# Two blocks of 96 columns of an fp32 MLP product made together from three packed weight sets

## The chip, the cores and the metric

The kernel runs on one core of a Trainium2 chip. The metric is the device time of one execution in microseconds (us); each version is run several times, and the median counts. A core has five engines that run side by side, each with its own queue of instructions: TensorE (matmuls, PE in the profile, with its weight loads as PEld), VectorE (DVE), ScalarE (ACT), GpSimd (POOL) and SyncE (SP), which issues most transfers from memory. Data lies in SBUF, with 128 partitions, and matmul results lie in PSUM, which is eight banks here used as four slots of two banks.

## The reference

The reference has two halves. The first gates a long causal convolution (a diagonal state space model) with the queries and adds it to the input. The second, which matters here, is a token-mixing MLP on 2048 tokens and 640 channels with F = 1728 hidden columns:

```python
h = _layernorm(x, axis=-1)                            # (B, S, D), then scaled and shifted
u = jnp.einsum("bsd,sf->bdf", h, w1) + b1             # 2048 tokens -> 1728 columns
u = _gelu(u)
y = jnp.einsum("bdf,fs->bds", u, w2) + b2             # 1728 columns -> 2048 tokens
```

All of it is in fp32. The change touches only the first of these two products.

## The kernel before

**Three matmuls for one.** TensorE is fed with the type fp32r, and each fp32 operand is split into a rounded high part and the rest ("lo"). The helper `mm` (L437 to L444) makes high x high, high x rest and rest x high, each in two halves of 320 columns: six matmuls of 128x128 weights for one block of 128 columns and one 128-token chunk. The product of the two rests is left out. The tokens come in 16 chunks `H[j]`, each a pair (high, rest) of 640 columns, so one block takes 96 matmuls.

**The blocks.** The 1728 hidden columns are cut into 14 blocks of 128, seven for each half of 864. Since 864 is six times 128 and 96 more, blocks 6 and 13 repeat 32 columns of the block before them and have 96 new ones (`fo`, L384). When such a block's result leaves PSUM, the mask `msk` sets its first 32 rows to zero (L850, L851).

**The order.** The program's order is written out by hand; waits follow from which tiles are read and written. Blocks 0 to 3 are made earlier, beside the second layer norm, in four accumulators. Then the loop at L899 runs over blocks 4 to 13. For each it first splits the next block's weights (`split_w`, L423: two ScalarE copies for the high part, L432, and two VectorE subtractions for the rest) and loads the one after that (`load_w`, L396: two transfers of 512 KB on SP), then issues the 96 matmuls, then the evacuation `u_evac` (L844): a gelu in place in PSUM on ScalarE (L847), and for each half of 320 columns a ScalarE copy and a VectorE subtraction into the tiles `U[f]`. Loads go into one raw tile `X`; split weights go into two tiles `T_wb` in turn, by the block's parity.

**The tiles.** A tile name stands for a place in SBUF, and a new tile in a place waits for all uses of the old one. The place "in" holds block 3's weights until TensorE is through with blocks 0 to 3, and then `u_i`, where results go. The place "p" holds `m_p`, with room for temporaries. PSUM slots are taken in a ring of four.

**After it.** In the last block's time, VectorE and ScalarE make sums of the results for a Strassen-like second product (`t_ops`, L863, for three of seven parts), and only then evacuate block 13. The second product starts with a plain loop over four column blocks of w2 (L1029 to L1052), each with 14 groups of six matmuls, one for each `U[f]` in order of f, and then runs 42 smaller products (L974).

Of the kernel before, what the change touches and what calls it, by code (L numbers as in the profile page):

```python
# [10 lines left out]
F32R = mybir.dt.float32r  # L11
AF = mybir.ActivationFunctionType
ALU = mybir.AluOpType
# [37 lines left out]
def mixer_kernel(ctx: ExitStack, tc: tile.TileContext, q, k, v, shift_k, ssm_k, ssm_D, w1, b1, w2, b2, c,  # L51
# [7 lines left out]
    act, dve, pool, pe, sync = nc.scalar, nc.vector, nc.gpsimd, nc.tensor, nc.sync  # L59
    TT = lambda eng, o, a, b, op: eng.tensor_tensor(o, a, b, op=op)  # L60
    uid = [0]

    def mem(tag, n, name=None):

        return sb.tile([128, n], F32, name=name or tag, tag=tag, bufs=1)
# [4 lines left out]
    def psum(slot=None):  # L70

        uid[0] += 1
        slot = ring[uid[0] % len(ring)] if slot is None else slot
        return psp.tile([128, 1024], F32, name=f"pst_{uid[0]}", tag=f"pst{slot}", bufs=1)

    def dram(t, offset, ap):
        return bass.AP(tensor=t.tensor, offset=t.offset + offset, ap=ap)
# [206 lines left out]
    def i1(half, slot=None):  # L284

        ps = psum(slot)
        for jj in range(8):
            for ri in range(2):
                for e in range(2):
                    p = slice(64 * e, 64 * e + 64)  # L290
                    for b in range(2):
                        n2 = 16 * b + 8 * half + jj
                        pe.matmul(ps[64 * b:64 * b + 64, 512 * e + 64 * jj:512 * e + 64 * jj + 64],  # L293
                                  V1[p, ri, n2], T2[p, :, 32 * ri + n2], start=ri == 0, stop=ri == 1)
        return ps
# [85 lines left out]


    NF, NW = 14, 4
    fo = lambda f: 864 * (f // 7) + min(128 * (f % 7), 736)  # L384
    raw, blk = {}, {}
    j16 = lambda t: t[:, 0:2048].rearrange("p (j m) -> p j m", j=16)
    f14 = lambda t: t[:, 0:1792].rearrange("p (f m) -> p f m", f=14)

    def load_w2(t, s, f0, n):

        for h in range(n // 7 or 1):
            o = 7 * h
            sync.dma_start(t[:, o:o + 6, :], dram(w2, fo(f0 + o) * S + 128 * s, [[S, 128], [128 * S, 6], [1, 128]]))
            sync.dma_start(t[:, o + 6, :], dram(w2, fo(f0 + o + 6) * S + 128 * s, [[S, 128], [1, 128]]))

    def load_w(i, t=X):  # L396
        if i >= NF + NW:
            return
        if i < NF:
            t = j16(t)  # L400
            for b in range(2):
                sync.dma_start(t[64 * b:64 * b + 64],
                               dram(w1, 16 * b * F + fo(i), [[32 * F, 64], [F, 16], [1, 128]]))
            raw[i] = (t, [slice(0, 8), slice(8, 16)])
        else:
            t = f14(t)
            load_w2(t, i - NF, 0, 14)
            raw[i] = (t, [slice(0, 7), slice(7, 14)])
# [12 lines left out]
            TT(dve, blk[f][1][:, j].bitcast(F32R), t[:, :, 128 * f:128 * f + 128], blk[f][0][:, j], ALU.subtract)  # L421

    def split_w(i, t2=None, eng=dve):  # L423
        if i >= NF + NW:
            return
        if t2 is None:
            t2 = T_wb[i % 2]
        view = j16 if i < NF else f14
        hi, lo = view(t2[:, 0:2048]), view(t2[:, 2048:4096])
        t, parts = raw.pop(i)  # L430
        for f in parts:
            act.activation(hi[:, f].bitcast(F32R), t[:, f], AF.Copy)  # L432
        for f in parts:
            TT(eng, lo[:, f].bitcast(F32R), t[:, f], hi[:, f], ALU.subtract)
        blk[i] = hi, lo

    def mm(ps, wh, wl, rh, rl, first, last, steps=None):  # L437

        m = wh.shape[-1]
        steps = steps or ((wh, rh), (wh, rl), (wl, rh))  # L440
        for i, (w_, r_) in enumerate(steps):
            for h in range(2):
                pe.matmul(ps[0:m, h, 0:320], w_.bitcast(F32R), r_[:, 320 * h:320 * h + 320].bitcast(F32R),  # L443
                          start=first and i == 0, stop=last and i == 2)  # L444
# [78 lines left out]
    for c in range(NC):  # L523
# [3 lines left out]
        for g in range(8):  # L527
            m_, a_ = f2(g)
# [35 lines left out]
        if c == 0:  # L564
# [3 lines left out]
            ps = psum()  # L568
# [45 lines left out]
        else:  # L614
# [6 lines left out]
            t = mem("in", 4288, "wb3")  # L621
# [4 lines left out]
        if c:  # L626
            dv(7 if cn is not None else 8)
            i2(0)
            if cn is None:
                mod_part(tap, 3, pl[3])  # L630
                i2(1, dve)
                t = mem("y", 4096, "wb2")
# [19 lines left out]
        for half in range(2):  # L652
            ps = i1(half)
# [15 lines left out]
        else:  # L669
# [3 lines left out]
    r_z, r_v = mem("z", 8192, "r_z"), mem("v", 4520, "r_v")  # L673
    unit = lambda t, n: [t[:, 1280 * i:1280 * i + 1280] for i in range(n)]
    H = (unit(r_z[:, 0:4096], 3) + unit(r_v, 3) + unit(mem("aux", 4096, "h_a"), 3)
         + unit(r_z[:, 3840:7680], 3))
# [14 lines left out]
    start = []  # L691
# [84 lines left out]
    ps = i1(1, s1)  # L776
# [34 lines left out]
    for pr in range(3, 8):  # L811
# [15 lines left out]
        if pr == 4:  # L827
# [5 lines left out]

    U = {}
    thirds = lambda t, n, o=0: [t[:, o + 320 * i:o + 320 * i + 320] for i in range(n)]
    u_i = mem("in", 4288, "u_i")
    left = [t_ for t, n in ((mem("t", 1280, "u_t"), 4), (mem("g", 1280, "u_g"), 4), (mem("kt", 1536, "u_k"), 4))
            for t_ in thirds(t, n)] + thirds(u_i, 1, 3840) + thirds(r_z, 1, 7680)
    right = thirds(mem("xb", 5120, "u_x"), 14)
    us = [left[2 * f:2 * f + 1] + right[2 * f:2 * f + 1] + left[2 * f + 1:2 * f + 2] + right[2 * f + 1:2 * f + 2]  # L840
          for f in range(7)]
    us += [thirds(t, 4, 1280 * i) for t in (u_i, mem("y", 4096, "u_y")) for i in range(3)]

    def u_evac(f, ps):  # L844
        u = U[f] = us[f] if f < 13 else [t[:, 320 * h:320 * h + 320] for t in H[15] for h in range(2)]
        p = ps[:, :, 0:320]
        act.activation(p, p, AF.Gelu_apprx_tanh, bias=B1C[:, f:f + 1])  # L847
        for h in range(2):
            if f % 7 == 6:
                act.activation(u[h].bitcast(F32R), p[:, h], AF.Copy, scale=msk)  # L850
                dve.scalar_tensor_tensor(u[2 + h].bitcast(F32R), p[:, h], msk, u[h], op0=ALU.mult, op1=ALU.subtract)  # L851
            else:
                act.activation(u[h].bitcast(F32R), p[:, h], AF.Copy)
                TT(dve, u[2 + h].bitcast(F32R), p[:, h], u[h], ALU.subtract)

    m_p = mem("p", 2048, "m_p")
    TU = [[(H[j][n][:, 0:320], H[j][n][:, 320:640]) for j in js for n in range(2)]
          for js in ((0, 1), (2, 6), (7, 8), (9, 10), (11, 12), (13, 14))]  # L860
    RB = thirds(m_p, 3, 1088)

    def t_ops(i, then=lambda: None):  # L863

        def whole(t, n, h):
            u = U[i + 7 * n]
            TT(dve, t, u[h], u[2 + h], ALU.add)
# [4 lines left out]
        def rest(n, t):  # L872
            TT(dve, TU[i][n][1].bitcast(F32R), t, TU[i][n][0], ALU.subtract)

        a, b, c_ = RB
        whole(a, 0, 0)
# [14 lines left out]
        rest(1, c_)  # L891
        rest(3, a)

    T_wb = [mem("w0", 4096, "wb0b"), mem("w1", 4096, "wb1b")]
    split_w(4)
    load_w(5)
    for f_ in range(4):
        u_evac(f_, acc[f_])
    for f_ in range(4, NF):  # L899
        ps = psum().rearrange("p (h m) -> p h m", h=2)  # L900
        split_w(f_ + 1)
        load_w(f_ + 2)
        for j in range(16):
            hh, hl = H[j]
            mm(ps, blk[f_][0][:, j], blk[f_][1][:, j], hh, hl, j == 0, j == 15)
        if f_ == NF - 1:
            m_v = mem("v", 4520, "m_v")
            for i in range(3):
                t_ops(i)
        u_evac(f_, ps)  # L910
# [4 lines left out]
    m_w, slots = [], []  # L915
# [105 lines left out]
    def early(s):  # L1021

        for h in range(2):
            o, x, b2_ = RB[h], xe[2 * s + h], B2C[:, s:s + 1]
            dve.scalar_tensor_tensor(o, acc[s][:, h, 0:320], b2_, GB[:, 320 * h:320 * h + 320], op0=ALU.add, op1=ALU.mult)
            TT(dve, x, o, x, ALU.add)
            sync.dma_start(out[128 * s:128 * s + 128, 320 * h:320 * h + 320], x)

    for s in range(NW):  # L1029
        i = NF + s  # L1030
        acc.append(psum().rearrange("p (h m) -> p h m", h=2))
        split_w(i + 1)
        load_w(i + 2)
        if s < 3:
            t_ops(3 + s)
        if s > 1:
            early(s - 2)
        if s == 3:
            load_pair(1, 0, 3)
            m_w.append(mem("w0", 4096, "m_w0"))  # L1040
            slots += [(q7(m_w[0], 1792 * i), q7(m_w[0], 1792 * i + 896)) for i in range(2)]
            prep(0)
            prep(1)
            sums(2)
            sums(3)
        wh, wl = blk[i]
        for f_ in range(NF):
            u = U[f_]
            for k, (w, r) in enumerate(((wh, 0), (wh, 2), (wl, 0))):
                for h in range(2):  # L1050
                    pe.matmul(acc[s][:, h, 0:320], w[:, f_].bitcast(F32R), u[r + h].bitcast(F32R),  # L1051
                              start=f_ == 0 and k == 0, stop=f_ == NF - 1 and k == 2)  # L1052
    m_w.append(mem("w1", 4096, "m_w1"))
    t_ = thirds(m_w[0], 1, 3584) + thirds(m_w[1], 7, 1792)
    TU.append([(t_[0], t_[1]), (t_[2], t_[3]), (t_[4], t_[5]), (t_[6], t_[7])])
    spare = thirds(mem("xb", 5120, "m_x"), 16)
# [57 lines left out]
```

## Time and profile before

| what | us |
|---|---|
| median of three runs | 712.46 |
| the three runs | 712.46, 717.07, 706.91 |
| span of the profiled execution | 705.8 |
| TensorE busy in it | 644.5 |
| VectorE busy | 492.5 |
| ScalarE busy | 307.1 |

The profile comes from one execution. Its span goes from the first instruction to the last; the execution's own time also holds what lies around that, which is not recorded for the profiled run, so the span stands beside the three runs. The mean granted clock of TensorE was 0.985 of full speed. Rows of the profile name the engine, the line, and the tile written and the tile read; `wb0b` and `wb1b` are the two tiles of split weights, `pst` is PSUM, `x` the raw tile. A busy time of TensorE does not say how fast its matmuls follow each other, since they overlap; their spacing is read from the length of a string of them and its count.

### The profile page before, as it was taken

The numbers are of one execution on the slowest core, as the hardware profiler recorded it, in microseconds if no ns is written. First come the engines' busy times: TensorE is split into PE (matmuls) and PEld (weight loads), VectorE is DVE, ScalarE is ACT, GpSimd is POOL, SyncE is SP. The second block draws the span as 40 slices with busy tenths as digits, with TensorE's granted clock in tenths as the row PEclk, the third lists the DMA queues.
The fourth block names the chain that finished last, engine by engine and source line by source line (L and its number), as shares of the span: only waits on it lengthen the run. The fifth ranks groups of instructions, "written<-read, shape, count | busy, mean of one in ns | idle before, by whom it ended". The sixth has DMA issues, their size and how long they took to land.

```text
span 705.8 us, 20785 instructions
## 1 busy us (share of the span) xinstructions
PE 644.5 (91%) x9131; PEld 624.2 (88%) x9131; DVE 492.5 (70%) x861; ACT 307.1 (44%) x473; POOL 155.9 (22%) x135
## 2 busy tenths in 40 slices
PE   0699779989999989977899999999999999999997
PEld 0699469889999989777899999999999999999997
DVE  7778468969879638888884312311298979888886
ACT  0664554645745645556767223222334322333331
POOL 5297039615526428100010000000000000000000
PEclk9999979999999999999999999999999999999999
DMA  9968978446333522361303543354163243555511
GB/s 180 219 205 238 350 148 168 110 76 144 68 62 88 172 59 68 115 150 30 60 1 60 99 82 60 61 103 77 52 194 105 88 149 99 166 170 170 148 60 38
DMA packets 166672, 82.80 MB, mean 117 GB/s; under 512 B 89235, under 2 KB 157622, under 8 KB 166582
## 3 DMA queue, kind: packets, MB, share of 16 engines
q1 hardware_dynamic: 162034, 80.17, 46.0%
q10 hardware_dynamic: 4548, 1.31, 1.1%
q8 instruction: 71, 1.16, 0.7%
q14 instruction: 19, 0.16, 0.1%
HBM read 70.97 MB, written 10.49 MB: 115 GB/s over the span
## 4 chain that ended last, share of the span: by engine, by line
PE 65%; DVE 16%; ACT 4%; DMA 4%; POOL 4%; issue 3%; SPq 2%; ACTq 0%; DVEq 0%; POOLq 0%
PE pst L443 21%; PE pst L974 17%; PE pst L1051 7%; PE pst L229 7%; PE pst L245 6%; PE pst L274 4%; POOL y L60 3%; DVE tap L60 3%; PE pst L293 2%; DVE kt L60 2%; DVE p L60 2%; DMA aux<-in_w_mod_dram 2%; SPq L163 2%; DVE aux L60 1%; DVE y L60 1%
## 5 line engine op out<-in xcount | busy, mean ns | idle before, releaser
L245 PEld LDWEIGHTS pst<-z,w 128*64 128x64 f32 x2560 | 94.6, 141 | 7.9 <-ACT z L231 7.3
L245 PE MATMUL pst<-z,w 128*64 128x64 f32 x2560 | 95.8, 240 | 6.2 <-ACT z L231 6.1
L60 POOL TENSOR_TENSOR y<-p 128x256 f32<-128x256 f32 x72 | 92.3, 1341 | 22.4 <-DVE p L60 21.9
L60 DVE TENSOR_TENSOR p<-pst,kt 128x512 f32<-128x512 f32 x80 | 52.4, 691 | 23.8 <-ACT kt L249 15.5
L229 PE MATMUL pst<-v,x 128*64 128x128 f32 x640 | 44.3, 297 | 23.6 <-DVE x L60 23.6
L231 ACT ACTIVATE z<-pst 128x1024 f32<-128x1024 f32 x40 | 45.9, 1148 | 42.7 <-PE pst L229 23.1
L229 PEld LDWEIGHTS pst<-v,x 128*64 128x64 f32 x640 | 42.5, 220 | 24.1 <-POOL t L468 23.5
L847 ACT ACTIVATE pst<-pst,sm 128x640 f32<-128x640 f32 x14 | 10.7, 767 | 85.7 <-PE pst L443 85.7
L249 ACT ACTIVATE kt<-pst 128x512 f32<-128x512 f32 x40 | 25.1, 627 | 47.4 <-PE pst L245 26.6
L274 PEld LDWEIGHTS pst<-v,y 32*128 32x128 f32 x1280 | 38.1, 187 | 6.7 <-POOL y L60 3.8
L229 PE MATMUL pst<-v,p 128*64 128x128 f32 x640 | 39.6, 282 | 4.2 <-issue 2.2
L274 PE MATMUL pst<-v,y 32*128 32x64 f32 x1280 | 40.0, 272 | 3.8 <-DVE y L60 2.7
L974 PE MATMUL pst<-r_z,m_w 128*128 128x320 f32 x222 | 41.6, 309 | 0.7 <-DVE m_w L60 0.7
L229 PEld LDWEIGHTS pst<-v,p 128*64 128x64 f32 x640 | 36.9, 142 | 5.6 <-issue 2.9
L962 ACT ACTIVATE m_w<-m_v 128x896 fp32r<-128x896 f32 x24 | 22.2, 949 | 38.5 <-DVE m_v L60 23.1
L60 DVE TENSOR_TENSOR tap<-tap,kt 128x512 f32<-128x512 f32 x51 | 35.6, 698 | 1.3
L60 DVE TENSOR_TENSOR kt<-in,tap 128x512 f32<-128x512 f32 x51 | 35.0, 686 | 1.5
L974 PEld LDWEIGHTS pst<-r_z,m_w 128*128 128x128 f32 x222 | 34.8, 188 | 0.9 <-DVE m_w L60 0.9
L60 DVE TENSOR_TENSOR m_w<-m_v,m_w 128x896 fp32r<-128x896 f32 x24 | 26.0, 1088 | 9.5 <-ACT m_w L962 9.5
L282 ACT ACTIVATE z<-pst 128x512 f32<-128x512 f32 x38 | 21.5, 670 | 23.2 <-PE pst L274 23.2
L962 ACT ACTIVATE m_w<-m_p 128x896 fp32r<-128x896 f32 x12 | 11.5, 954 | 41.2 <-DVE m_p L60 24.4
L443 PE MATMUL pst<-r_z,wb0b 128*128 128x320 f32 x180 | 28.1, 310 | 0.9 <-DVE u_x L60 0.9
(278 smaller groups left out, 1436.9 us busy)
## 6 DMA issues: line engine op xcount, KB each, us to landing
x<-in_B_w_dram SPq DMA_DIRECT2D x22, 512.0 KB
m_v<-in_B_w_dram SPq DMA_DIRECT2D x15, 384.0 KB
x<-in_B_w_dram SPq DMA_DIRECT2D x14, 384.0 KB
aux<-in_A_ssm_k_dram SPq DMA_DIRECT2D x10, 512.0 KB
in<-in_A_k_dram SPq DMA_DIRECT2D x36, 128.0 KB
in<-in_A_v_dram SPq DMA_DIRECT2D x36, 128.0 KB
m_x<-xs SPq DMA_DIRECT2D x28, 160.0 KB
out_dram<-m_x SPq DMA_DIRECT2D x28, 160.0 KB
```

Of the source, the lines that this page charges most:

```text
L60: TT = lambda eng, o, a, b, op: eng.tensor_tensor(o, a, b, op=op)
L163: sync.dma_start(KSR[64 * h:64 * h + 64].rearrange("p (i n) -> p i n", i=64), dram(ssm_k, (DC * c + 64 * h) * S, [[32, 64], [S, 64], [1, 3 ...
L229: pe.matmul(ps[64 * ri:64 * ri + 64, o:o + 128], lhs, F1[:, 128 * ri:128 * ri + 128], start=True, stop=True)
L231: evac = lambda: act.activation(Z[:, side, t].rearrange("p a k e -> p e a k"), ps.rearrange("p (e a k) -> p e a k", a=8, e=2), AF.Copy)
L245: pe.matmul(ps[64 * h:64 * h + 64, o:o + 64], W2[k1 // 32][:, 2 * (k1 % 32) + ri], rhs, start=True, stop=True)
L249: act.activation(kt.rearrange("p (m i) -> p m i", i=32), pv[:, :, 1], AF.Copy)
L274: pe.matmul(pp[qd // 2][:, o:o + 64], Y[p, ri, i:i + 2].rearrange("p i k -> p (i k)"), V2[p, 64 * ri:64 * ri + 64], start=ri == 0, stop=ri ...
L282: act.activation(o, i, AF.Copy)
L443: pe.matmul(ps[0:m, h, 0:320], w_.bitcast(F32R), r_[:, 320 * h:320 * h + 320].bitcast(F32R), start=first and i == 0, stop=last and i == 2)
L962: act.activation(W[n][0].bitcast(F32R), A[p, w_], AF.Copy)
L974: pe.matmul(bank[n], w[:, i].bitcast(F32R), r.bitcast(F32R), start=i == 0 and k == 0, stop=i == 6 and k == 2)
L1051: pe.matmul(acc[s][:, h, 0:320], w[:, f_].bitcast(F32R), u[r + h].bitcast(F32R), start=f_ == 0 and k == 0, stop=f_ == NF - 1 and k == 2)
```

## The change

Blocks 6 and 13 leave the loop, which now runs over 4 to 12. Their weight parts are packed into three sets of 128 columns. Each of the first two has 96 columns of a high part (block 6, block 13) and 32 columns of block 13's rest; the third has the 96 columns of block 6's rest and the last 32 of block 13's. The first two sets are multiplied with the high and the rest part of every chunk, the third with the high part only: five products in place of six. The results lie in three PSUM slots. ScalarE copies the three pieces of block 13's rest (partitions 0 to 31 of each slot) side by side into a temporary, VectorE adds that to the second slot, ScalarE copies the third slot out, and VectorE adds it to the first. Then both blocks are evacuated as before.

To have both blocks' weights at hand, block 6 is loaded earlier, into the place "in", and block 13 where block 6 was. The three sets are split in block 5's time (`split_ends`), and made and joined (`ends`) between blocks 5 and 7. The two weight tiles change hands by position in the new order, no longer by parity, and the tiles `u_i` and `m_p` are taken only after the three sets are done. The last block before the second product is now block 12, and it gets the result tiles that block 13 had.

```diff
+    FS = (4, 5, 6, 7, 8, 9, 10, 11, 12)
+    WB = {i: n % 2 for n, i in enumerate(FS + tuple(range(NF, NF + NW)))}
...
-            t2 = T_wb[i % 2]
+            t2 = T_wb[WB[i]]
...
-    u_i = mem("in", 4288, "u_i")
+    raw6 = mem("in", 2048, "raw6")
...
+    us[12] = [t[:, 320 * h:320 * h + 320] for t in H[15] for h in range(2)]
...
     split_w(4)
     load_w(5)
     for f_ in range(4):
         u_evac(f_, acc[f_])
-    for f_ in range(4, NF):
+    load_w(6, raw6)
+    raw6_ = raw.pop(6)[0]
...
+    def split_ends():
+
+        t13 = raw.pop(13)[0]
+        sets = [j16(t_) for t_ in (T_wb[0][:, 0:2048], T_wb[0][:, 2048:4096], mem("p", 2048, "ends"))]
+        parts = [slice(0, 8), slice(8, 16)]
+        for t, s_ in ((raw6_, sets[0]), (t13, sets[1])):
+            for f in parts:
+                act.activation(s_[:, f, 32:128].bitcast(F32R), t[:, f, 32:128], AF.Copy)
+        for f in parts:
+            TT(dve, sets[2][:, f, 32:128].bitcast(F32R), raw6_[:, f, 32:128], sets[0][:, f, 32:128], ALU.subtract)
+        for n in range(3):
+            o = slice(32 + 32 * n, 64 + 32 * n)
+            TT(dve, sets[n][:, :, 0:32].bitcast(F32R), t13[:, :, o], sets[1][:, :, o], ALU.subtract)
+        return sets
+
+    def ends(sets):
+
+        ps = [two_(psum()) for _ in range(3)]
+        for j in range(16):
+            hh, hl = H[j]
+            for n, r in ((0, hh), (0, hl), (1, hh), (1, hl), (2, hh)):
+                for h in range(2):
+                    pe.matmul(ps[n][:, h, 0:320], sets[n][:, j].bitcast(F32R),
+                              r[:, 320 * h:320 * h + 320].bitcast(F32R), start=j == 0 and r is hh,
+                              stop=j == 15 and (n == 2 or r is hl))
+        m_p, u_i = mem("p", 2048, "m_p"), mem("in", 4288, "u_i")
...
+        t = two_(m_p[:, 0:640])
+        dve.memset(m_p[0:32, 0:640], 0.0)
+        for n in range(3):
+            act.activation(t[32 + 32 * n:64 + 32 * n], ps[n][0:32, :, 0:320], AF.Copy)
+        a6, a13, a_ = (p[:, :, 0:320] for p in (ps[0], ps[1], ps[2]))
+        TT(dve, a13, a13, t, ALU.add)
+        act.activation(t, a_, AF.Copy)
+        TT(dve, a6, a6, t, ALU.add)
+        u_evac(13, ps[1])
+        u_evac(6, ps[0])
+        return m_p
+
+    for f_ in FS:
+        n_ = nxt(f_)
+        if f_ == 5:
+            sets = split_ends()
+        else:
+            split_w(n_)
+        load_w(13 if f_ == 4 else nxt(n_))
+        if f_ == 6:
+            m_p = ends(sets)
+            continue
         ps = psum().rearrange("p (h m) -> p h m", h=2)
-        split_w(f_ + 1)
-        load_w(f_ + 2)
         for j in range(16):
             hh, hl = H[j]
             mm(ps, blk[f_][0][:, j], blk[f_][1][:, j], hh, hl, j == 0, j == 15)
-        if f_ == NF - 1:
+        if f_ == FS[-1]:
             m_v = mem("v", 4520, "m_v")
             for i in range(3):
                 t_ops(i)
...
-            m_w.append(mem("w0", 4096, "m_w0"))
+            m_w.append(mem(f"w{WB[NF + 2]}", 4096, "m_w0"))
```

`nxt(i)` gives the block whose weights follow those of block i in the new order (4, 5, 6, 7, ... 12, then the four blocks of w2).

More of the change, by code (lines that the diff above doesn't have):

```diff
@@ L396, in load_w @@
     def load_w(i, t=X):
-        if i >= NF + NW:
+        if i is None:
             return
@@ L423, in split_w @@
     def split_w(i, t2=None, eng=dve):
-        if i >= NF + NW:
+        if i is None:
             return
         if t2 is None:
-            t2 = T_wb[i % 2]
+            t2 = T_wb[WB[i]]
         view = j16 if i < NF else f14
@@ L835, in mixer_kernel @@
     thirds = lambda t, n, o=0: [t[:, o + 320 * i:o + 320 * i + 320] for i in range(n)]
-    u_i = mem("in", 4288, "u_i")
+    raw6 = mem("in", 2048, "raw6")
     left = [t_ for t, n in ((mem("t", 1280, "u_t"), 4), (mem("g", 1280, "u_g"), 4), (mem("kt", 1536, "u_k"), 4))
-            for t_ in thirds(t, n)] + thirds(u_i, 1, 3840) + thirds(r_z, 1, 7680)
+            for t_ in thirds(t, n)]
     right = thirds(mem("xb", 5120, "u_x"), 14)
-    us = [left[2 * f:2 * f + 1] + right[2 * f:2 * f + 1] + left[2 * f + 1:2 * f + 2] + right[2 * f + 1:2 * f + 2]
-          for f in range(7)]
-    us += [thirds(t, 4, 1280 * i) for t in (u_i, mem("y", 4096, "u_y")) for i in range(3)]
+    quarters = lambda f: (left[2 * f:2 * f + 1] + right[2 * f:2 * f + 1] + left[2 * f + 1:2 * f + 2]
+                          + right[2 * f + 1:2 * f + 2])
+    us = {f: quarters(f) for f in range(6)}
+    us[12] = [t[:, 320 * h:320 * h + 320] for t in H[15] for h in range(2)]
     def u_evac(f, ps):
-        u = U[f] = us[f] if f < 13 else [t[:, 320 * h:320 * h + 320] for t in H[15] for h in range(2)]
+        u = U[f] = us[f]
         p = ps[:, :, 0:320]
@@ L854, in u_evac @@
                 TT(dve, u[2 + h].bitcast(F32R), p[:, h], u[h], ALU.subtract)
-    m_p = mem("p", 2048, "m_p")
     TU = [[(H[j][n][:, 0:320], H[j][n][:, 320:640]) for j in js for n in range(2)]
           for js in ((0, 1), (2, 6), (7, 8), (9, 10), (11, 12), (13, 14))]
-    RB = thirds(m_p, 3, 1088)
+    RB = []
     def t_ops(i, then=lambda: None):
@@ L892, in t_ops @@
         rest(3, a)
+    two_ = lambda t: t.rearrange("p (h m) -> p h m", h=2)
     T_wb = [mem("w0", 4096, "wb0b"), mem("w1", 4096, "wb1b")]
@@ L898, in mixer_kernel @@
         u_evac(f_, acc[f_])
-    for f_ in range(4, NF):
+    load_w(6, raw6)
+    raw6_ = raw.pop(6)[0]
+    after = dict(zip(FS, FS[1:] + tuple(range(NF, NF + NW))))
+    after.update({i: i + 1 for i in range(NF, NF + NW - 1)})
+    nxt = lambda i: after.get(i)
+    def split_ends():
[11 more added lines that the diff above has]
+        return sets
@@ new lines, in ends @@
+    def ends(sets):
[8 more added lines that the diff above has]
+        m_p, u_i = mem("p", 2048, "m_p"), mem("in", 4288, "u_i")
+        left.extend(thirds(u_i, 1, 3840) + thirds(r_z, 1, 7680))
+        us[6] = quarters(6)
+        us.update(zip((7, 8, 9, 10, 11, 13), [thirds(t, 4, 1280 * i) for t in (u_i, mem("y", 4096, "u_y"))
+                                              for i in range(3)]))
+        RB.extend(thirds(m_p, 3, 1088))
+        t = two_(m_p[:, 0:640])
[9 more added lines that the diff above has]
+        return m_p
@@ L1031, in mixer_kernel @@
         acc.append(psum().rearrange("p (h m) -> p h m", h=2))
-        split_w(i + 1)
-        load_w(i + 2)
+        split_w(nxt(i))
+        load_w(nxt(nxt(i)))
         if s < 3:
@@ L1052, in mixer_kernel @@
                               start=f_ == 0 and k == 0, stop=f_ == NF - 1 and k == 2)
-    m_w.append(mem("w1", 4096, "m_w1"))
+    m_w.append(mem(f"w{WB[NF + 3]}", 4096, "m_w1"))
     t_ = thirds(m_w[0], 1, 3584) + thirds(m_w[1], 7, 1792)
```

## The prediction

> **What bounds the kernel.** I read the head and the slices of the page first, then the chain that ended last, from 376 us on.
>
> ```profile
> span 705.8 us, 20785 instructions
> ...
> PE 644.5 (91%) x9131; PEld 624.2 (88%) x9131; DVE 492.5 (70%) x861; ACT 307.1 (44%) x473; POOL 155.9 (22%) x135
> ...
> PEld 0699469889999989777899999999999999999997
> DVE  7778468969879638888884312311298979888886
> ...
> PEclk9999979999999999999999999999999999999999
> ```
>
> ```profile
> 381.03 141.06 PE pst L443 x960
> 522.10 49.31 PE pst L1051 x336
> 571.40 6.17 PE pst L974 x42
> ...
> 584.69 117.15 PE pst L974 x796
> ```
>
> In the slices (each 17.6 us) TensorE's weight loads, one per matmul, stand at nine tenths or more from the 21st on (the last aside), at the full granted clock, while VectorE moves between 1 and 9. The chain (start, us, what) says the same in order of time: from 381.03 us on it is a string of matmuls, 960 of the first MLP product (L443), 336 of the second (L1051), then the products of L974. Its few steps on other engines lie between 577 and 585 us. Whether TensorE stands still inside the string is told by the windows (length, busy time by engine, then granted clock, DMA share and GB/s):
>
> ```profile
> 381.00:577.00 196.00, 195.97 (x1336) 195.97 (x1337) 90.64 (x151) 61.16 (x97) 0.00 (x0) 1.00 0.42 97
> 577.00:585.00 8.00, 7.33 (x50) 7.07 (x50) 7.22 (x14) 1.28 (x2) 0.00 (x0) 1.00 0.47 159
> 585.00:701.00 116.00, 116.00 (x792) 115.89 (x791) 100.03 (x144) 38.75 (x48) 0.00 (x0) 1.00 0.41 122
> ```
>
> In 196 us TensorE is idle for 0.03, and later for 0.67 in all. So in this stage the end is set by the number of matmuls, and what VectorE, ScalarE and the loads do there is free as long as each weight block is ready when its turn comes. The price of a matmul is 141.06 us / 960 = 146.9 ns. The change acts only in this stage; all before 380 us stays.
>
> **What it takes away.** Blocks 6 and 13 now cost 2 x 16 x 6 = 192 matmuls, and the five products of three sets cost 2 x 16 x 5 = 160, of the same shape (128x128 weights, 320 columns). 32 x 146.9 ns = 4.70 us, all on the path. No other matmul changes. Two things could alter the price of the 160: they rotate over three accumulators, and a set serves four, four and two matmuls in a row. The stage before shows both kinds of rotation, with matmuls going round four accumulators in groups of four and two:
>
> ```profile
> 356.83 8.41 PE L443 MATMUL pst<-r_z,wb 128*128 128x320 f32 x56
> 365.81 14.33 PE L443 MATMUL pst<-h_x,wb 128*128 128x320 f32 x96 [0.57 <-ACT h_x L742]
> 381.03 1.14 PE L443 MATMUL pst<-r_z,wb0b 128*128 128x320 f32 x6 [0.90 <-DVE u_x L60]
> ```
>
> ```profile
> 356.83:365.24 8.41, 8.41 (x58) 8.15 (x56) 7.84 (x18) 6.51 (x14) 0.90 (x1) 1.00 0.01 2
> ```
>
> 56 matmuls in 8.41 us, of which the last one's 0.31 is its own length: 8.10/55 = 147.3 ns, at clock 1.00. The string of L974, which changes weights after two and one, gives 117.15/796 = 147.2. So the price holds within 0.5 ns, 0.08 us for the 160.
>
> [...]
>
> **What it adds beside TensorE, block by block.** A block lasts 96 x 146.9 ns = 14.1 us. The time order around blocks 4 and 5 shows how such a block's helpers run (start, length, engine, line, operation):
>
> ```profile
> 386.74 2.00 ACT L432 ACTIVATE wb1b<-x 128x1024 fp32r<-128x1024 f32 x2
> ...
> 387.83 2.36 DVE L60 TENSOR_TENSOR wb1b<-x,wb1b 128x1024 fp32r<-128x1024 f32 x2 [0.46 <-ACT wb1b L432]
> ...
> 390.22 1.31 SPq L402 DMA_DIRECT2D x<-in_B_w_dram  x2
> ```
>
> ```profile
> 395.22 2.80 PE L443 MATMUL pst<-r_z,wb1b 128*128 128x320 f32 x18
> 395.42 0.77 ACT L847 ACTIVATE pst<-pst,sm 128x640 f32<-128x640 f32 x1 [6.68 <-PE pst L443]
> ...
> 397.21 0.44 ACT L853 ACTIVATE u_x<-pst 128x320 fp32r<-128x320 f32 x1 [0.56 <-DVE u_k L60]
> 397.68 0.49 DVE L60 TENSOR_TENSOR u_x<-pst,u_x 128x320 fp32r<-128x320 f32 x1 [0.50 <-ACT u_x L853]
> ...
> 397.85 2.01 ACT L432 ACTIVATE wb0b<-x 128x1024 fp32r<-128x1024 f32 x2 [0.20 <-DMA x<-in_B_w_dram]
> ...
> 398.94 2.36 DVE L60 TENSOR_TENSOR wb0b<-x,wb0b 128x1024 fp32r<-128x1024 f32 x2 [0.77 <-ACT wb0b L432]
> ...
> 409.30 2.80 PE L443 MATMUL pst<-r_z,wb0b 128*128 128x320 f32 x18
> ```
>
> Block 4's result leaves in 395.42 to 398.17 (ScalarE is done at 397.65). Block 6 was loaded at 390.22, just after VectorE had finished with the raw tile (390.19), had landed by 397.85, since ScalarE waited 0.20 for it, and was split by 401.30. Block 6's turn came at 409.30: 8.0 us of cover.
>
> The earlier load: block 5's raw data is asked for when VectorE has ended split 4, in this row.
>
> ```profile
> 375.99 2.36 DVE L60 TENSOR_TENSOR wb0b<-x,wb0b 128x1024 fp32r<-128x1024 f32 x2 [2.30 <-ACT wb0b L432]
> ```
>
> Block 6 is now loaded into the old "in" tile, queued behind block 5's load on SP; it has to wait until TensorE has done with that tile, 380.1 (365.81 + 14.33). Behind it on SP stands only block 13's load, which waits for block 5's split anyway. Both loads (1 MB each) move at once. One load took at most 397.85 - 390.22 = 7.63 us. At worst the second doubles the first: block 5 lands at 378.4 + 2 x 7.63 = 393.7 at the very latest (issued at 375.99 + 2.36 = 378.35) and splits in 3.45 us, 397.1, against its turn at 395.2: that would be 1.9 us of stall, or about 0, as block 5 starts with its first half. I take 0: block 5's load is ahead in the one queue, and its split began without a DMA wait at 386.74, which leaves 5.0 us until it would be late (386.74 + 3.45 = 390.2 against 395.2).
>
> Making the sets, in block 5's time, behind block 4's evacuation. I need rows for other sizes:
>
> ```profile
> L60 DVE TENSOR_TENSOR p<-pst,kt 128x512 f32<-128x512 f32 x80 | 52.4, 691 | 23.8 <-ACT kt L249 15.5 <-POOL y L60 8.0
> ...
> L60 DVE TENSOR_TENSOR tap<-tap,kt 128x512 f32<-128x512 f32 x51 | 35.6, 698 | 1.3
> ...
> L60 DVE TENSOR_TENSOR wb1b<-x,wb1b 128x1024 fp32r<-128x1024 f32 x10 | 11.8, 1222 | 2.3 <-ACT wb1b L432 2.3
> ...
> L432 ACT ACTIVATE wb1b<-x 128x1024 fp32r<-128x1024 f32 x10 | 10.0, 1050 | 0.0
> ...
> L60 DVE TENSOR_TENSOR wb1b<-x,wb1b 128x896 fp32r<-128x896 f32 x4 | 4.2, 1088 | 0.5 <-ACT wb1b L432 0.5
> ...
> L432 ACT ACTIVATE wb1b<-x 128x896 fp32r<-128x896 f32 x4 | 3.6, 940 | 0.0
> ```
>
> From 1024 to 896 elements ScalarE gains 110 ns and VectorE 134, so 768 take 0.83 and 0.95. ScalarE: 4 x 0.83 = 3.3. VectorE: 2 x 0.95 for the rest of block 6, and three pieces of 16 x 32 = 512 elements; the row p<-pst,kt also has runs of 32 (its swapped operand, L255) and takes 0.69, so 2.1; together 4.0. ScalarE's copies of block 13 wait for its load; behind them stands only block 5's evacuation, not due before 409.3. From 397.65 that ends near 402.5, or near 405.5 if block 13 lands 3 us later. The turn is at 409.3: covered by 4 to 7 us. Against two whole splits it costs the engines nothing that shows.
>
> Putting the results together, in the time of block 7, after the 160 matmuls (T is their end): one memset, three ScalarE copies of 32 partitions x 640, VectorE add, ScalarE copy 128x640, VectorE add, then two evacuations, all before split 8 in the queues. Its nearest rows:
>
> ```profile
> L357 ACT ACTIVATE t<-tap x1: 707/707/707, 297.0 to 297.0; 96x640 f32<-96x640 f32 x1
> ```
>
> ```profile
> L449 DVE MEMSET g<- x1: 165/165/165, 0.8 to 0.8; 36x128 f32 x1
> ```
>
> ```profile
> 529.06 0.75 ACT L847 ACTIVATE pst<-pst,sm 128x640 f32<-128x640 f32 x1
> 529.84 0.53 ACT L850 ACTIVATE h_x<-pst,sm 128x320 fp32r<-128x320 f32 x1
> ...
> 531.42 1.78 ACT L432 ACTIVATE wb1b<-x 128x896 fp32r<-128x896 f32 x2
> ```
>
> Copies: 0.71 each (96 partitions, the same length), 2.1. Memset 0.17 and beside them. Add: the row tap<-tap,kt also reads and writes PSUM, 698 ns at 512, and with 1.05 ns per element more 0.83 at 640. Copy 0.71. The second add runs beside the first gelu. So ScalarE begins the evacuations at T + 0.1 + 2.1 + 0.83 + 0.71 = T + 3.8. An evacuation of a masked block holds it from 529.06 to 531.42, 2.4 us: two, T + 8.6. Split 8 takes 3.45 (397.85 to 401.30): T + 12.0. Block 8's turn is T + 14.1. Covered by 2.1 us, and by 3.2 if only the first half of the rest has to be there (its two halves take 2.36 together). These rows are the thinnest cover of the change: their lower end is that all is hidden; their upper end, if the five new steps that follow one another (three copies, an add, a copy: 3.7 us) took twice as long, is 3.7 - 2.1 = 1.6 us of stall. No gain can come of them. I take 0, since lengths set the rows (0.71 at 96 partitions, 0.77 for the gelu at 128). What waits: ScalarE's first copy and VectorE's memset write where the third set lay, so both wait for T; behind them in their queues stand the two evacuations and split 8, and only block 8 waits for those. GpSimd and SP are not involved. The next load goes out at T + 12 rather than some T + 6, lands 7.6 later, T + 19.6, and its split ends by T + 23.1 against T + 28.2: the delay does not pass on.
>
> The tail: the last block is now 12 and the second product wants it as its 13th group, not its 14th:
>
> ```profile
> 531.56 0.55 DVE L851 SCALAR_TENSOR_TENSOR h_x<-pst,sm,h_x 128x320 fp32r<-128x320 f32 x1 [0.60 <-ACT h_x L850]
> ...
> 533.38 1.04 PE L1051 MATMUL pst<-h_x,wb0b 128*128 128x320 f32 x6
> ```
>
> Block 13 was complete at 532.11 and read at 533.38; block 12 will be read 6 matmuls, 0.88 us, earlier relative to that, 0.39 us after 532.11, and its evacuation without the mask is shorter (0.44 for 0.53 and 0.49 for 0.55, twice: 0.3 us). Cover 0.7 us; without it, a stall of as much as is lacking. The two weight tiles merely change names afterwards.
>
> **Sum.** -4.70, and 0 for all the rest: span 705.8 - 4.7 = 701.1. The quickest of the three runs, 706.91, is 1.1 above the span, so the profiled execution is like that run and 5.6 below the median. I forecast the median: 712.46 - 4.7 = 707.8, 0.66% less.
>
> **Rivals.** All hidden, the forecast: -4.7, 707.8. For it: the windows without idle time, and every cover above. Chance 0.78.
>
> Partly paid back (the second load stalls block 5, the joining block 8, or the tail the second product, by 1 to 4.5 us): 708.8 to 712.3. For it: the covers of 2.1 and 0.7 us, and 1.9 us lacking in the worst case of the load; against it: a block starts on its first half. 0.12.
>
> The joining becomes the bound, and the kernel gets slower. It decides from the point where the five steps take 3.7 + 2.1 + 4.7 = 10.5 us, 2.8 times as much. At four times, 14.8, block 8 waits 14.8 - 3.7 - 2.1 = 9.0 and the time is 712.46 - 4.7 + 9.0 = 716.8. For it: copies from partitions 0 to 31 into another 32 have no row; against it: every row goes by its length. It passes 2% only beyond six times. 0.04.
>
> [...] 0.02. [...]
>
> The change doesn't do what it says: the loops give 160 matmuls, so it could only be that something I have not seen gives the 4.7 us back or adds to them, up to the spread of the runs either way: 712.5 in the middle, 0.04.
>
> **Range and chances.** The three runs of the one kernel differ by 10.2 us, more than the gain. Less 4.7 they lie from 702.2 to 712.4; with 1 us for what is paid back at the upper end and half a microsecond of it below: 701.5 to 713.5. 2% of 712.46 is 14.2 us, about what a measurement of this kernel can tell from no change, and three times the gain. Faster by more: only by the spread, 0.03. Slower by more: rotation, the far end of the joining, an unseen effect, 0.05. Within: 0.92.
>
> **What would show it.** In the profile after: 928 matmuls of L443 and its new line between 381 us and the second product, which would begin at 517.4; 146.9 ns each and clock 1.00 in the 160; TensorE idle under 0.1 us in that stretch; split 8 done about 12 us after the 160th; block 7's evacuation not late. Wrong would be idle time of TensorE ended by ScalarE or VectorE at block 5, the sets, block 8 or the 13th group of the second product, or a matmul price over 148 ns in the three accumulators.

## The result and the profile after

| | before | after |
|---|---|---|
| median of 20 runs, us | 709.79 | 705.52 |
| lowest and highest run, us | 703.62, 723.14 | 702.53, 712.44 |
| ratio, 95% interval | | 0.9957 [0.9939, 0.9975] |
| span of the profiled execution, us | 705.8 | 703.0 |

The changed kernel is faster, by 4.27 us by the medians (0.60%) and by 0.43% [0.25, 0.61] by the ratio; the forecast was 4.7 us, 0.66%. The two measures differ because the ratio leaves out runs more than 1.5% above the fastest of their own kernel, and these are six of the twenty before and none of the twenty after.

The head of the page after and the slices of TensorE's granted clock (tenths, 17.6 us each):

```profile
span 703.0 us, 20726 instructions
...
PEclk9999978999999999989889999999999999999999
```

From the 23rd slice on it shows a 9 throughout, as before; from 387 us to the end the clock was 1.00. Ahead of that the 7th slice and, between 316 and 387 us, the 19th, 21st and 22nd show an 8 where the page before showed a 9.

The chain that ended last, from block 4 on (start us, us, what). L445 is the line of `mm`, which was L443; L930 is the new line of the 160 matmuls, L1110 the second product:

```profile
382.81 28.43 PE pst L445 x192
411.24 23.53 PE pst L930 x160
434.77 84.48 PE pst L445 x576
519.25 49.31 PE pst L1110 x336
```

From block 4 to the second product it is 519.25 - 382.81 = 136.44 us, and it was 141.06: 4.62 us less. The 160 matmuls take 23.53 us, 147.1 ns each. The window over this stretch (length, busy time of PE, PEld, DVE, ACT, POOL, clock, DMA share, GB/s) shows TensorE idle for 0.01 us, with VectorE busy for a third of the time:

```profile
382.80:519.00 136.20, 136.19 (x928) 136.19 (x929) 44.93 (x67) 42.91 (x67) 0.00 (x0) 1.00 0.45 93
```

But block 4 begins at 382.81, and it began at 381.03: before it, where the two programs have the same work, this execution lost 1.78 us, and so the span shows 2.8 us and not 4.6. Whether that belongs to the change is the question of the first experiments.

The time order in block 5's time shows the three sets being made (start, length, engine, line, operation, out<-in), in two extracts; `raw` is block 6's raw tile, `ends` the third set:

```profile
388.51 2.00 ACT L434 ACTIVATE wb1b<-x 128x1024 fp32r<-128x1024 f32 x2
...
391.98 1.31 SPq L404 DMA_DIRECT2D x<-in_B_w_dram  x2
```

```profile
399.33 1.57 ACT L915 ACTIVATE wb0b<-raw 128x768 fp32r<-128x768 f32 x2
...
400.20 1.83 DVE L60 TENSOR_TENSOR ends<-raw,wb0b 128x768 fp32r<-128x768 f32 x2 [0.24 <-ACT wb0b L915]
400.80 1.57 ACT L915 ACTIVATE wb0b<-x 128x768 fp32r<-128x768 f32 x2
...
402.40 1.29 DVE L60 TENSOR_TENSOR wb0b<-x,wb0b 128x512 fp32r<-128x512 f32 x2 [0.38 <-ACT wb0b L915]
403.62 0.68 DVE L60 TENSOR_TENSOR ends<-x,wb0b 128x512 fp32r<-128x512 f32 x1
...
411.08 1.34 PE L930 MATMUL pst<-r_z,wb0b 128*128 128x320 f32 x8
```

Split 5 begins at 388.51 with no wait for its load. Block 13, asked for at 391.98, is there when ScalarE comes to it at 400.80, since no wait for a transfer stands in that row. The sets are whole at 403.62 + 0.68 = 404.30, and the first of the 160 matmuls begins at 411.08: 6.8 us of cover, where the prediction had 4 to 7.

After the 160 matmuls the results are joined, in block 7's time:

```profile
434.61 2.80 PE L445 MATMUL pst<-r_z,wb1b 128*128 128x320 f32 x18
434.81 2.10 ACT L942 ACTIVATE m_p<-pst 32x640 f32<-32x640 f32 x3 [19.41 <-PE pst L930]
434.96 0.59 DVE L940 MEMSET m_p<- 32x640 f32 x1 [18.11 <-PE pst L930]
436.95 0.83 DVE L60 TENSOR_TENSOR pst<-pst,m_p 128x640 f32<-128x640 f32 x1 [1.39 <-ACT m_p L942]
...
437.81 0.71 ACT L945 ACTIVATE m_p<-pst 128x640 f32<-128x640 f32 x1 [0.90 <-DVE pst L60]
438.42 0.76 ACT L850 ACTIVATE pst<-pst,sm 128x640 f32<-128x640 f32 x1
...
443.16 2.00 ACT L434 ACTIVATE wb0b<-x 128x1024 fp32r<-128x1024 f32 x2
...
444.24 2.36 DVE L60 TENSOR_TENSOR wb0b<-x,wb0b 128x1024 fp32r<-128x1024 f32 x2 [0.40 <-ACT wb0b L434]
...
448.69 2.80 PE L445 MATMUL pst<-r_z,wb0b 128*128 128x320 f32 x18
```

With T = 434.61, ScalarE begins the evacuations at T + 3.8, split 8 begins at T + 8.6 and ends at 444.24 + 2.36 = 446.60, T + 12.0, and block 8 begins at T + 14.1. The three copies of 32 partitions, which had no row before, take 0.70 us each, and the adds that read and write PSUM 0.83.

The last rows that the prediction used are those of the last block's result and of its reader, the 13th group of the second product:

```profile
528.46 0.49 DVE L60 TENSOR_TENSOR h_x<-pst,h_x 128x320 fp32r<-128x320 f32 x1 [0.50 <-ACT h_x L856]
...
529.66 1.04 PE L1110 MATMUL pst<-h_x,wb1b 128*128 128x320 f32 x6
```

The result is whole at 528.95 and read at 529.66: 0.71 us of cover.

### The profile page after: what moved, and what is told of

It is laid out like the page before. It is cut to its first block, busy times and chain, and to the rows that moved or that the text cites. A ratio compares the mean times of both kernels' runs of the same rounds, so it can differ in the third digit from the quotient of the medians.

```text
span 703.0 us, 20726 instructions
## 1 busy us (share of the span) xinstructions
PE 643.0 (91%) x9099; PEld 623.8 (89%) x9099; DVE 494.3 (70%) x865; ACT 307.9 (44%) x477; POOL 155.7 (22%) x135
## 4 chain that ended last, share of the span: by engine, by line
PE 69%; DVE 14%; DMA 6%; POOL 4%; ACT 3%; issue 3%; SPq 1%; ACTq 0%; DVEq 0%; POOLq 0%
PE pst L445 20%; PE pst L1033 18%; PE pst L229 8%; PE pst L1110 7%; PE pst L245 6%; PE pst L274 4%; POOL y L60 4%; PE pst L930 3%; DVE tap L60 2%; DMA aux<-in_A_ssm_k_dram 2%; PE pst L293 2%; DVE kt L60 2%; DMA aux<-in_w_mod_dram 2%; DVE aux L60 2%; DVE p L60 1%
## 5 line engine op out<-in xcount | busy, mean ns | idle before, releaser
L293 PEld LDWEIGHTS pst<-z,v 64*64 64x64 f32 x1280 | 22.4, 144 | 7.6 <-issue 4.9
```

## The experiments

Theory A says that the change is worth its 32 matmuls and nothing else, and that the 1.78 us are scatter of the part before block 4. Theory B says that the rest of the change costs 1.2 to 1.8 us. All ratios are to the kernel before, run in the same session.

**The kernel before, once more,** with no edit.

> The kernel before, unchanged, run once more. Theory A (the change is worth exactly its 32 matmuls, and what the ratio lacks to that is the scatter of the part before block 4): the string of matmuls from block 4 to the second product again lasts 141.06 us within 0.1, but its start, 381.03 in the first profile, moves by up to 2 us; ratio 1.000 within its interval. Theory B (the change costs 1.8 us before block 4, where the profiles differ by 382.81 - 381.03): the start stays within 0.3 us of 381.0.

Measured: 708.77 us against 708.56 (medians), ratio 1.0012 [0.9989, 1.0035]. The chain of this execution:

```profile
381.62 141.06 PE pst L443 x960
```

The string is 141.06 us to the hundredth; its start moved by 0.59 us. This alone does not reach 1.78.

**The changed kernel, once more,** with no edit.

> The changed kernel once more, beside the next one on the same chip. Theory A: 382.8 or elsewhere at the start, but 136.44 us from block 4 to the second product; ratio to before 0.9935 (32 matmuls are 4.7 of 709) within its interval. Theory B (1.6 us lost elsewhere): ratio 0.9957 again.

Measured: 704.92 us against 708.98 (medians), ratio 0.9948 [0.9919, 0.9977], which holds the forecast's 0.9934 and the first 0.9957.

```profile
380.06 28.42 PE pst L445 x192
408.48 23.53 PE pst L930 x160
...
516.49 49.31 PE pst L1110 x336
```

Here block 4 begins at 380.06, earlier than in either profile of the kernel before, and the string is 516.49 - 380.06 = 136.43 us. So the 1.78 us do not belong to the change. Over all profiles, with the same work up to that point apart from one instruction in the two kernels with the early table, block 4 begins anywhere from 380.06 to 388.71 us. Where it is latest (the set-by-set kernel, below), the granted clock between 290 and 320 us was 0.72, and in the profile of the changed kernel that began earliest it was 1.00:

```profile
290.00:320.00 30.00, 27.20 (x511) 21.98 (x507) 20.19 (x43) 11.99 (x23) 0.64 (x3) 0.72 0.33 86
```

```profile
290.00:320.00 30.00, 23.46 (x484) 20.22 (x482) 25.27 (x58) 15.04 (x30) 1.04 (x5) 1.00 0.40 90
```

In another late one, 388.44 us in the kernel with four copies more (below), it was 0.94 there and 0.93 in the long stretch ahead of it:

```profile
120.00:290.00 170.00, 159.79 (x4060) 154.22 (x4057) 123.92 (x210) 86.47 (x139) 81.99 (x64) 0.93 0.39 91
290.00:320.00 30.00, 26.75 (x617) 21.31 (x612) 25.67 (x50) 16.48 (x32) 3.28 (x6) 0.94 0.47 127
```

The first profile of the kernel before, which began at 381.03, also had 0.94 between 290 and 320 us, but 1.00 between 120 and 290. So the three latest starts, 388.71, 388.44 and 386.06 us (the last in the kernel with the early table, below, at 0.73 between 290 and 320), come with the lowest clock in one of these two stretches. Among the other starts the clock gives no order: the kernel with the sets split late (below) began at 380.94 and the changed kernel at 382.81, both with 0.89 between 290 and 320. Whether the lower clock is the cause, or itself the trace of waits of TensorE, as in two experiments below, was not tried, nor what makes it differ from one execution to the next.

**The sixth product put back:** the packing, the loads and the joining stay, but the third set also multiplies the rests of the tokens.

```diff
-            for n, r in ((0, hh), (0, hl), (1, hh), (1, hl), (2, hh)):
+            for n, r in ((0, hh), (0, hl), (1, hh), (1, hl), (2, hh), (2, hl)):
...
-                              stop=j == 15 and (n == 2 or r is hl))
+                              stop=j == 15 and r is hl)
```

> The changed kernel with the sixth product put back (the third set also times the rest of the tokens), so 192 matmuls between blocks 5 and 7 with the packing, the loads and the joining all kept. Theory A: the 32 matmuls are all the gain: 28.2 us for the 192, the string from block 4 to the second product 141.1 us, ratio 1.000 (0.998 to 1.002). Theory B (the rest of the change costs about 1.6 us): ratio 1.002 or more. Rival (the new order itself gains something): ratio below 0.998.

Measured: 708.57 us against 708.56, ratio 0.9997 [0.9973, 1.0021].

```profile
381.53 28.43 PE pst L445 x192
409.96 28.23 PE pst L930 x192
...
522.66 49.31 PE pst L1110 x336
```

The 192 take 28.23 us, 4.70 more than the 160, and the string is 522.66 - 381.53 = 141.13, 0.07 more than before. All that surrounds the 32 matmuls costs 0.07 us in the string, and the ratio shows no more, within 0.24% (1.7 us) either way. Theory A stands.

**Set by set:** all chunks for the first set, then the second, then the third, so that the matmuls don't go round three accumulators.

```diff
-        for j in range(16):
-            hh, hl = H[j]
-            for n, r in ((0, hh), (0, hl), (1, hh), (1, hl), (2, hh)):
-                for h in range(2):
+        for n in range(3):
+            for j in range(16):
+                hh, hl = H[j]
+                for r, h in ((hh, 0), (hh, 1), (hl, 0), (hl, 1))[:2 if n == 2 else 4]:
```

> The changed kernel with the 160 matmuls set by set (all 16 chunks for the first set, then the second, then the third), so no rotation over three accumulators. If rotation cost nothing, 23.5 us again and a time within 0.2% of the changed kernel (ratio to before about 0.995). [...]

Measured: 703.84 us against 708.56, ratio 0.9953 [0.9924, 0.9982].

```profile
417.14 23.46 PE pst L930 x160
```

23.46 us against 23.53: the rotation costs 0.07 us, which is the 0.07 that the kernel with six products was over. In the profile after, the granted clock was 1.00 over all of the 160, from 411.24 to 434.77 us.

**A longer joining:** the copy of the third slot is issued 15 times, to see where its cover ends.

```diff
-        act.activation(t, a_, AF.Copy)
+        for _ in range(15):
+            act.activation(t, a_, AF.Copy)
```

> The changed kernel with the ScalarE copy of the third slot issued 15 times in place of once, 14 x 0.70 = 9.8 us more in the joining. If the cover is what the prediction had (2.1 us for the whole split of block 8, about 3.2 if a block starts on its first half), TensorE waits for block 8 between 9.8 - 3.2 - 0.6 = 6.0 us (first half) and 7.7 us (whole), and the time rises by as much over the changed kernel. If block 8 does not depend on the joining, no wait.

Measured: 712.55 us against 708.75, ratio 1.0046 [1.0027, 1.0064]. The chain, the time order of the copies and of block 8's start, and the windows at and after the wait:

```profile
383.22 28.43 PE pst L445 x192
...
527.39 49.31 PE pst L1111 x336
```

```profile
438.22 11.02 ACT L946 ACTIVATE m_p<-pst 128x640 f32<-128x640 f32 x15 [0.90 <-DVE pst L60]
...
454.96 4.66 PE L445 MATMUL pst<-r_z,wb0b 128*128 128x320 f32 x18 [5.70 <-ACT wb0b L434]
```

```profile
449.00:455.00 6.00, 0.30 (x3) 0.04 (x2) 3.09 (x6) 4.70 (x9) 0.00 (x0) 0.74 0.00 0
455.00:458.00 3.00, 3.00 (x11) 2.77 (x12) 2.71 (x3) 2.21 (x4) 0.00 (x0) 0.50 0.00 0
458.00:462.00 4.00, 4.00 (x27) 4.00 (x27) 0.49 (x1) 0.18 (x1) 0.00 (x0) 0.92 0.88 185
```

Block 8 waits 5.70 us, for ScalarE's first half of the high part, so it does begin on its first half. The 15 copies took 11.02 us where the one took 0.71, 10.31 more and not 9.8, so the cover was 10.31 - 5.70 = 4.6 us and not 3.2: block 8 begins once the first half of the high part is there, ahead of the first half of the rest, from which the 3.2 was worked out. The whole stretch grew more than the wait, though: from 383.22, where block 4 began in this execution, to 527.39 it is 144.17 us, 7.73 over 136.44. The first 18 matmuls of block 8 take 4.66 us where they took 2.80, with the granted clock at 0.50 between 455 and 458. The wait lies below both bounds, 6.0 and 7.7; the loss reaches the upper one only because of a slower clock, which neither had in it.

**Four copies more** instead of 14, between the two covers (`range(5)` in the same edit).

> The changed kernel with the ScalarE copy of the third slot issued 5 times in place of once: 4 x 0.73 = 2.9 us more in the joining. If block 8 has to wait for its whole split, the string from block 4 to the second product grows by 2.9 - 2.1 = 0.8 us, 136.44 to 137.2; if it starts on its first half, the cover is 3.2 and the string stays at 136.44.

Measured in one profiled execution (710.79 us):

```profile
388.44 28.43 PE pst L445 x192
...
524.88 49.31 PE pst L1111 x336
```

524.88 - 388.44 = 136.44 us: no wait. Split 8 ended in this execution after block 8 had begun:

```profile
452.81 2.36 DVE L60 TENSOR_TENSOR wb0b<-x,wb0b 128x1024 fp32r<-128x1024 f32 x2 [0.40 <-ACT wb0b L434]
...
454.32 2.80 PE L445 MATMUL pst<-r_z,wb0b 128*128 128x320 f32 x18
```

It ends at 455.17, 0.85 us after block 8's first matmul at 454.32, and TensorE has no idle time in front of that row. A block starts on the first half of its split.

**The sets split late:** the same instructions, but the split of the three sets stands behind block 5's evacuation in the queues, and block 7's load and split behind it.

```diff
-        if f_ == 5:
-            sets = split_ends()
-        else:
-            split_w(n_)
-        load_w(13 if f_ == 4 else nxt(n_))
+        if f_ == 6:
+            sets = split_ends()
+            load_w(n_)
+        if f_ != 5:
+            split_w(n_)
+            load_w(13 if f_ == 4 else nxt(n_))
```

> The changed kernel with the same instructions, but the three sets split behind block 5's evacuation in the queues in place of ahead of it (the load of block 7 and its split go behind them). Theory: the gain rests on the sets being made in block 5's time; now TensorE waits for evacuation 5 and for the sets: about 6.1 us before the 160 matmuls (the first set is ready 3.7 us after ScalarE begins, which is 2.3 us after block 5's end), time 1.5 us above before, ratio about 1.002. Rival: the split is cheap enough to hide in the evacuation's gaps, wait under 3 us.

Measured: 711.32 us against 708.75, ratio 1.0027 [1.0006, 1.0047].

```profile
415.34 2.50 PE L930 MATMUL pst<-r_z,wb0b 128*128 128x320 f32 x8 [5.97 <-DVE wb0b L60]
```

```profile
415.34 25.76 PE pst L930 x160
441.10 84.48 PE pst L445 x576
```

The wait is 5.97 us (6.1 expected), and the 160 matmuls take 25.76 us, 2.23 more than with no wait ahead of them; again the clock stood at 0.50 after the wait (409.4 to 415.4), here for about 4 us. The eight matmuls of the row above take 2.50 us, and the eight that begin at 420.34 take 1.34. So the 0.74 below, from 418.4 to 421.0, is taken as a mean over the change; if the clock went from 0.50 straight to 1.00, it did so at 418.4 + 2.6 x 0.26 / 0.50 = 419.8, an estimate:

```profile
409.40:415.40 6.00, 0.06 (x1) 0.06 (x1) 3.62 (x6) 4.57 (x7) 0.00 (x0) 0.79 0.01 1
415.40:418.40 3.00, 3.00 (x11) 3.00 (x12) 1.09 (x2) 0.00 (x0) 0.00 (x0) 0.50 0.13 21
418.40:421.00 2.60, 2.60 (x15) 2.60 (x15) 0.00 (x0) 0.00 (x0) 0.00 (x0) 0.74 1.16 251
421.00:425.00 4.00, 4.00 (x29) 4.00 (x28) 0.25 (x1) 1.34 (x2) 0.00 (x0) 1.00 0.50 86
```

The place of the split in the queues alone is worth 5.97 + 2.23 = 8.2 us, nearly twice what the change gains.

**The gelu table loaded early:** TensorE's one wait at the start of this stage, 0.90 us before block 4, is at the end of a chain of split 4, the table load and block 0's evacuation. One gelu of one column ahead of split 4 takes the table load out of it.

```diff
+    act.activation(tm[:, 0:1], epsc, AF.Gelu_apprx_tanh)
     split_w(4)
```

> The changed kernel with one gelu of one column issued ahead of split 4, so that the gelu table is loaded while ScalarE would wait for TensorE anyway. The chain to block 4's start (split 4, table load 1.28 us, gelu of block 0, copies) becomes 1.28 us shorter, and TensorE's wait of 0.90 us before block 4 should vanish: ratio 0.001 below the changed kernel's, about 0.994 to 0.995. Rival: the wait is set by something else (VectorE's queue), and stays at 0.90.

Measured: 703.39 us against 708.56, ratio 0.9932 [0.9906, 0.9958]. The rows of the changed kernel and then of this one:

```profile
378.70 1.28 ACT L850 ACT_TABLE_LOAD   x1
...
382.81 2.91 PE L445 MATMUL pst<-r_z,wb0b 128*128 128x320 f32 x18 [0.90 <-DVE u_x L60]
```

```profile
378.78 1.28 ACT L898 ACT_TABLE_LOAD   x1
...
380.98 2.01 ACT L434 ACTIVATE wb0b<-x 128x1024 fp32r<-128x1024 f32 x2 [0.70 <-PE pst L445]
...
386.06 2.80 PE L445 MATMUL pst<-r_z,wb0b 128*128 128x320 f32 x18
```

The table load now lies ahead of split 4, whose own wait for TensorE shrinks to 0.70, and block 4's row has no idle time in front. Run again beside the changed kernel:

> The changed kernel with the gelu table loaded early, once more. TensorE's wait before block 4 is 0.00 in place of 0.90, and the ratio is 0.0013 below that of the changed kernel in the same session, if its interval lets that be seen.

702.41 us against 704.92 for the changed kernel and 708.98 before; ratio 0.9927 [0.9889, 0.9965] against 0.9948 [0.9919, 0.9977]. The wait is gone in the profiles; that the time is lower than the changed kernel's fits both sessions, but the intervals overlap. By the medians it is the fastest of the three, 6.57 us under the kernel before.

## Why the prediction was right

**The bound.** TensorE sets the end of this stage. The string has the same 141.06 us in both profiles of the kernel before and 136.43 to 136.44 in the profiles of the changed one.

**The 32 matmuls.** 4.70 us was forecast, and the kernel with six products shows 28.23 - 23.53 = 4.70 for them. On the path 4.62 is left (141.06 - 136.44), less 0.07 for the rotation, which had been given at most 0.08; the last 0.01 is within the rounding of the rows.

**The covers.** No step of what was added shows on the path. The sets were ready 6.8 us ahead (4 to 7 forecast), split 8 was done 2.1 us before block 8 (2.1), and the last result 0.7 us before its reader (0.7). Block 5's split had no wait for its load. The memset took 0.59 us, not 0.17, and lay beside the copies as said. The second figure for the joining, 3.2 us of cover on the first half, was too small: the kernel with 15 copies shows 4.6, and in the kernel with four copies more, 2.9 us added, nothing waited. The worst case of the earlier load, in which a second load doubles the first, was not seen: in the profile after, block 5's load was asked for at 380.15 and block 6's at 381.94, and ScalarE began split 5 at 388.51 with no wait for it, so it took at most 8.36 us with the second load behind it, where the prediction had read at most 7.63 for one alone.

**The rivals.** Partly paid back: not seen. The joining as the bound: it does turn the change into a loss when it is long enough, as the kernel with 15 copies shows, but the five steps took 2.10 + 0.83 + 0.71 us and their waits, as in the forecast. Rotation, which has its share in the chance of a slower kernel: no run shows a lower clock by it. The 160 took 23.53 us, at a clock of 1.00, and 23.46 set by set, so it cost 0.07.

**What was mis-sized.** The price of a wait was too small: the forecast put a stall of block 8 at its own length, but the waits of 5.70 and 5.97 us went with 2.03 and 2.23 us more, in matmuls at a clock of 0.50 after them. The cover of the joining was too small as well: 4.6 us, not 2.1 or 3.2. In the rival of the slower kernel the two errors nearly cancel. With the joining at four times its length, 11.1 us more, block 8 would wait 11.1 - 4.6 = 6.5 us in place of 9.0, and with some 2.0 for the clock lose 8.5, an estimate from the kernel with 15 copies. Neither changes the forecast, in which nothing waits.

**The total.** The median after, 705.52, lies 2.3 us below the forecast of 707.8, since the twenty runs of the kernel before have a median of 709.79, not the 712.46 of the first three. Of the change itself, the medians show 4.27 (20 runs), 4.06 (again) and 4.72 (set by set). The ratios, 0.9957, 0.9948 and 0.9953, show 0.4 to 0.5%, which is 3.1 to 3.7 us; the first's interval just leaves out 0.9934, the other two hold it. Where the missing microsecond can lie is narrow: the strings agree to 0.01 us, from the second product to the end all eleven profiles take 183.7 to 183.8 us, and every run whose span is on record took 2.1 to 2.2 us more than its span. So it would have to come before block 4, where the executions scatter. That it is scatter and no cost of the change is argued: the kernel with six products, which has all the rest of the change, leaves room for 1.7 us either way.

The same 2.1 us correct one reading of the prediction. It set the profiled execution of the kernel before at 706.9 us, like the quickest run; with a span of 705.8 it took about 707.9, so 4.6 and not 5.6 below the median of the three runs.

## What to carry to other kernels

Where one engine is busy without a gap, the price of an edit is its count on that engine times the spacing of its instructions in a long string (here 32 x 146.9 ns = 4.70 us, where the strings show 4.62), and everything else is worth checking only against its due time: list, for each thing that is prepared beside it, when it is ready and when its turn comes. An instruction's place in the queue can be worth more than the instruction: the same split, put behind an evacuation, cost 8.2 us, where the change gains 4.6. And where runs scatter by more than the gain, measure the stretch that the edit touches in the profile: it repeated to 0.01 us while whole runs differed by 10.

## What was not expected of the hardware

After a wait of TensorE of 5.70 us (block 8, in the kernel with 15 copies) and of 5.97 us (the 160 matmuls, in the kernel with the sets split late) the granted clock was 0.50: from 455 to 458 us in the first, from 415.4 to 418.4 in the second. After the 0.90 us before block 4 in the profile after it stayed at 1.00 (380 to 386 us). When it changed at these two waits is an estimate from the means of the windows next to these, taken as if the clock had only been 1.00 or 0.50: with 0.74 between 449 and 455 and 0.92 between 458 and 462, it fell some 2.6 us into the first wait and was back some 3.7 us after it; with 0.79 between 409.4 and 415.4 and 0.74 between 418.4 and 421, it fell some 3.5 us into the second and was back some 4.4 us after it. Waits of a length between 0.90 and 5.70 us were not tried in this stage. The extra cost was 7.73 - 5.70 = 2.03 us in the first case and 25.76 - 23.53 = 2.23 in the second.

The same work before block 4 ended at times 8.65 us apart (380.06 to 388.71) from one execution to another, and the two latest had a granted clock of 0.72 between 290 and 320 us, or of 0.93 between 120 and 290. That is nearly twice what the change gains.
